# Pooled attention values on 64 zero-padded rows and four array quarters, copied out in four pieces

## The chip, the cores and the metric

The kernel runs on one core of one Trainium2 chip. The metric is the device time of one execution in microseconds (us); of several executions the median counts. The core has four engines that compute, each with its own queue of instructions: PE (the matmul array, whose weight loads are shown as an engine of their own, PEld), DVE (vector), ACT (activations and copies) and POOL. SP issues the transfers. Each engine works through its queue in the order of the program and waits at an instruction until what it needs is there.

## What is computed

Attention with two parts, and two dense layers behind it. The part that the change touches is the pooled one: queries, keys and values of 576 positions are averaged in groups of four to 144, full attention runs on these, and each result is repeated four times.

```python
q_d = q.reshape(B, H, Sd, factor, D).mean(axis=3)     # B, H = 8, 8; Sd = 144; D = 64
k_d = k.reshape(B, H, Sd, factor, D).mean(axis=3)
v_d = v.reshape(B, H, Sd, factor, D).mean(axis=3)
out_d = sm_attn(q_d, k_d, v_d)                        # softmax(q_d k_d^T / 8) v_d
out_up = np.repeat(out_d, factor, axis=2)
...
out_local = np.matmul(attn, v)                        # attention to positions at most 3 away
x = (out_up + out_local)                              # heads side by side: 4608 x 512
h = x @ w_in                                          # 512 -> 2048
return np.maximum(0.01 * h, h) @ w_out                # 2048 -> 512
```

## The kernel before

**The dense layers** take most of PE's time. The 4608 tokens are cut into chunks of 256, 320 and 384 (`CHUNKS`). For each chunk and each of 16 slices of the hidden layer, `up_proj` (L862) makes 12 matmuls into a bank `hp`, ACT and DVE form `gh` and `gl` from it (`leaky`, L872, L873, L875), and `down_proj` (L902) makes 12 matmuls into the four banks `acc0` to `acc3`.

**The attention** of batches 1 to 7 runs beside them. Two heads that lie in the partitions 0 to 63 and 64 to 127 of a tile are a head pair `c`; `pair(b, u)` handles the two head pairs `cs = 2u, 2u + 1`, so four heads, and runs 14 times (7 batches, 2 values of `u`). In the program below, `p` is the half of the partitions (which head of a head pair) and `i` the head pair of the two. The steps of `pair`:

- loads of queries and keys (`qk`) and of values (`vs`), with sums over four positions on DVE: `qk_d` (L499) and `v_d` (L511). The 144 pooled keys are held as three groups `kc` of 48; a head's group stands in 48 rows from row 0 or from row 64 of the tile. `KROWS` is 64 + 48 = 112.
- scores (L524): 12 matmuls over `qi`, `i`, `p`, each on 64 rows (the head's) and 64 columns of the array: rows by `p`, columns by `i`. All four quarters of the array are used in turn.
- softmax: maxima and reciprocals on DVE (L453, L454, L470, L471), exponentials and scaling on ACT (L463, L539), into `pds`. `pds` keeps 64 places for each group of 48 keys; the 16 places left over are zeros, written once by POOL at the start (L268).
- transposes (L548): nine per call, three for each `kc`, which put the keys on the partitions; ACT copies them to `ptd` (L551).
- values (L565): 12 matmuls over `i`, `kc`, `p`, each on the 48 rows of a head and 64 columns, which are the first 64 columns for all; the heads `p` have a bank each (`avs[p]`), the head pairs `i` stand side by side in it, 144 columns each.
- two ACT copies (L571), one for each bank, 64 partitions by 288, into `outd`. The sums that follow are `widen` (L808) and `landing` (L821, L828, L834, L836), which puts the attention's result into the input tiles `xh`, `xl` of the dense layers.

**Order.** All of this is written as generators. A planner (`Order`) keeps a time for each engine from stated costs and issues whichever step can start first; that fixes the program's order on each engine, and the chip runs it as written. The planner's costs of the steps in `pair` (`pe(1.1, ...)`, `op("ACT", 288, ...)`) are the same before and after the change, and one step issues all of its instructions together.

## Time and profile before

| | |
|---|---|
| median of three executions | 949.75 us (947.03 to 952.76) |
| the profiled execution | 951.45 us, its span 949.7 us |
| mean clock granted to PE | 0.987 of full speed |
| matmuls of scores, L524 | 336 records in 14 calls |
| matmuls of values, L565 | 336 records in 14 calls |

The profile tells, for one execution, when each instruction started and how long it took; the span is the time from its first to its last instruction. A matmul on 32-bit floats leaves two records, so that the 12 matmuls of a call are 24. Durations of matmuls include the way through the array and overlap, so that a row's duration is no distance: how long a block holds the engine is read from the start of its first matmul to the start of the next matmul behind it. Rows in the form `start, duration, engine line` are from the timeline, with the idle time before an instruction and what ended it in square brackets.

### The profile page before, as it was taken

To read this page: it belongs to the slowest core of one execution; us is meant where nothing else is said; L and a number is where in the kernel's file an instruction comes from. 1 tells how busy PE (TensorE), PEld (TensorE's weight loads), DVE (VectorE), ACT (ScalarE), POOL (GpSimd) and SP (SyncE) were. 2 spreads that over 40 slices of the span, in tenths; PEclk is the share of its full clock that TensorE was granted. 3 is DMA by queue.
4 is the path that set the end of the run, shared out by engine and by line. 5 is a ranking of instruction groups with operands and counts; after the bars stand their busy time and mean duration, and the time that the engine had idled before them with its cause. 6 is when DMAs were issued, how large, how long until landed. Compare 5 with 4: busy or idle time off the path is not lost.

```text
span 949.7 us, 16334 instructions
## 1 busy us (share of the span) xinstructions
PE 920.9 (97%) x6352; PEld 893.2 (94%) x6352; DVE 571.9 (60%) x897; ACT 414.2 (44%) x1133; POOL 610.1 (64%) x364
## 2 busy tenths in 40 slices
PE   6898999998899999999999999999999999999997
PEld 4688999898899999999999999999999999999997
DVE  4785866786676776568765776666665654311111
ACT  3777655553454454335543535343423423422211
POOL 4455867778767868787797687887888885100000
PEclk9699999999999999999999999999999999999999
DMA  9769556536333552333624452443332421000000
GB/s 243 240 210 330 174 158 209 178 109 192 124 112 97 181 161 82 111 119 123 199 82 131 129 168 84 128 130 96 113 99 77 149 60 51 34 1 1 34 1 34
DMA packets 60286, 117.60 MB, mean 124 GB/s; under 512 B 5472, under 2 KB 32864, under 8 KB 60208
## 3 DMA queue, kind: packets, MB, share of 16 engines
q1 hardware_dynamic: 60208, 116.55, 39.3%
q8 instruction: 50, 0.82, 0.4%
q14 instruction: 28, 0.23, 0.1%
HBM read 106.57 MB, written 9.96 MB: 123 GB/s over the span
## 4 chain that ended last, share of the span: by engine, by line
PE 90%; DMA 5%; DVE 2%; ACT 2%; issue 1%; SPq 0%; POOL 0%; DVEq 0%; POOLq 0%; ACTq 0%
PE acc L902 41%; PE hp L862 41%; PE pt L565 2%; PE pt L821 1%; PE pt L524 1%; DMA k<-in_w_in_dram 1%; PE pt L548 1%; DMA k<-in_kb_dram 1%; DMA su_vs<-in_vd_dram 1%; DMA w<-in_w_out_dram 1%; DMA vs<-in_vs_dram 1%; DVE s L729 0%; PE pt L624 0%; SPq L258 0%; ACT pds L463 0%
## 5 line engine op out<-in xcount | busy, mean ns | idle before, releaser
L723 POOL TENSOR_TENSOR prod<-q,k 128x1344 f32<-128x1344 f32 (+1 forms) x88 | 260.1, 2958 | 41.2 <-DMA k<-in_kb_dram 28.1
L784 POOL TENSOR_TENSOR prod<-v,s 128x1344 f32<-128x1344 f32 (+1 forms) x88 | 262.6, 2985 | 16.4 <-DMA v<-in_vb_dram 7.1
L872 ACT ACTIVATE gh<-hp 128x384 fp32r<-128x384 f32 (+2 forms) x208 | 97.4, 468 | 353.4 <-PE acc L902 334.4
L875 DVE TENSOR_TENSOR gl<-hp,gh 128x384 fp32r<-128x384 f32 (+2 forms) x208 | 108.8, 525 | 225.2 <-ACT hp L873 223.7
L862 PE MATMUL hp<-xh,w 128*128 128x384 f32 (+2 forms) x832 | 215.7, 327 | 0.0
L902 PE MATMUL acc<-gh,w 128*128 128x384 f32 (+2 forms) x832 | 215.5, 327 | 0.0
L862 PEld LDWEIGHTS hp<-xh,w 128*128 128x128 f32 x832 | 147.9, 188 | 1.2 <-issue 1.0
L902 PEld LDWEIGHTS acc<-gh,w 128*128 128x128 f32 x832 | 147.7, 188 | 1.2 <-issue 1.0
L862 PE MATMUL hp<-xh,wih 128*128 128x384 f32 (+2 forms) x416 | 139.7, 336 | 4.4 <-DVE gl L875 4.4
L790 DVE TENSOR_REDUCE xloc<-prod 128x192 f32<-128x1344 f32 (+1 forms) x88 | 130.0, 1477 | 13.9 <-POOL prod L784 13.8
L902 PE MATMUL acc<-gh,woh 128*128 128x384 f32 (+2 forms) x416 | 136.7, 328 | 1.4 <-ACT o L943 1.4
L729 DVE TENSOR_REDUCE s<-prod 128x21 f32<-128x1344 f32 (+1 forms) x88 | 130.1, 1479 | 11.4 <-POOL prod L723 11.2
L862 PE MATMUL hp<-xl,wih 128*128 128x384 f32 (+2 forms) x416 | 135.3, 325 | 0.8 <-DVE xl L836 0.8
L862 PE MATMUL hp<-xh,wil 128*128 128x384 f32 (+2 forms) x416 | 135.4, 326 | 0.0
L902 PE MATMUL acc<-gh,wol 128*128 128x384 f32 (+2 forms) x416 | 134.4, 323 | 0.4 <-POOL wol L341 0.4
L862 PE MATMUL hp<-xl,w 128*128 128x384 f32 (+2 forms) x416 | 134.8, 324 | 0.0
L902 PE MATMUL acc<-gl,w 128*128 128x384 f32 (+2 forms) x416 | 134.6, 324 | 0.0
L902 PE MATMUL acc<-gl,woh 128*128 128x384 f32 (+2 forms) x416 | 134.1, 322 | 0.0
L873 ACT ACTIVATE hp<-hp 128x384 f32<-128x384 f32 (+2 forms) x208 | 96.1, 462 | 0.0
L862 PEld LDWEIGHTS hp<-xh,wih 128*128 128x128 f32 x416 | 79.3, 191 | 7.9 <-DVE gl L875 5.6
L902 PEld LDWEIGHTS acc<-gh,woh 128*128 128x128 f32 x416 | 78.3, 188 | 3.0 <-ACT o L943 1.6
L862 PEld LDWEIGHTS hp<-xl,wih 128*128 128x128 f32 x416 | 79.3, 191 | 1.1 <-DVE xl L836 1.1
(172 smaller groups left out, 1228.7 us busy)
## 6 DMA issues: line engine op xcount, KB each, us to landing
k<-in_kb_dram SPq DMA_DIRECT2D x38, 576.0 KB, 4.3
v<-in_vb_dram SPq DMA_DIRECT2D x38, 576.0 KB, 4.8
qk<-in_qkt_dram SPq DMA_DIRECT2D x32, 576.0 KB, 5.8
vs<-in_vs_dram SPq DMA_DIRECT2D x56, 144.0 KB, 5.1
q<-in_qb_dram SPq DMA_DIRECT2D x38, 192.0 KB, 2.8
out_dram<-o SPq DMA_DIRECT2D x36, 192.0 KB, 2.0
w<-in_w_out_dram SPq DMA_DIRECT2D x6, 512.0 KB, 6.6
w<-in_w_in_dram SPq DMA_DIRECT2D x6, 512.0 KB, 7.7
```

What stands on the lines that cost most here:

```text
L524: nc.tensor.matmul(scs[p][outs, qi * SD:(qi + 1) * SD], qk_d[i][rows, qi * QB:qi * QB + 64], qk_d[i][rows, SD:2 * SD], start=True, stop=True)
L548: nc.tensor.transpose(tp[:KROWS, qi * 128:qi * 128 + KROWS], pds[:KROWS, qi, kc].rearrange("q p k -> q (p k)")[:, :KROWS], id_sb[:KROWS, : ...
L565: nc.tensor.matmul(avs[p][:64, i * SD:(i + 1) * SD], v_d[rows, i, kc], ptd[rows, kc, i], start=kc == 0, stop=kc == KC - 1)
L723: nc.gpsimd.tensor_tensor(out=prv, in0=q[:, p, a - j0:z - j0].unsqueeze(2).to_broadcast([128, n, W, D]), in1=view(k[:, p], (a - j0) * D, [ ...
L729: nc.vector.tensor_reduce(out=s[:, p, a - j0:z - j0], in_=prv, axis=AX.X, op=ALU.add)
L784: nc.gpsimd.tensor_tensor(out=prv, in0=view(v[:, p], a - j0, [[1, n], [nv, D], [1, W]]), in1=s[:, p, a - j0:z - j0].unsqueeze(2).to_broadc ...
L790: nc.vector.tensor_reduce(out=xl_t[:, :n, p], in_=prv, axis=AX.X, op=ALU.add)
L862: nc.tensor.matmul(hp[:, :n], wt[:, c], x[:, c], start=k == 0, stop=k == 3 * NC - 1)
L872: nc.scalar.activation(out=gh[:, :n], in_=hp[:, :n], func=AF.Prelu, alpha=0.01)
L873: nc.scalar.activation(out=hp[:, :n], in_=hp[:, :n], func=AF.Prelu, alpha=0.01)
L875: nc.vector.tensor_tensor(out=gl[:, :n], in0=hp[:, :n], in1=gh[:, :n].bitcast(F32), op=ALU.subtract)
L902: nc.tensor.matmul(acc[:, :n], wt[:, es], g[:, :n], start=f == f0 and j == 0, stop=f == f1 - 1 and j == 2)
```

## The change

The values' matmuls run on 64 rows for each head in place of 48: `v_d`, `vs` and `ptd` have 128 partitions, the rows 48 to 63 and 112 to 127 hold zeros (`vs` is cleared at the start, and the places that `pds` leaves free are carried through the transposes). The second head pair's results go to the columns 64 to 127 of the array, so to the partitions 64 to 127 of the banks, in place of 144 further columns of the first 64 partitions. The loop over `kc` is the outer one now, and within it the four quarters follow in the order in which the scores use them. Since a bank's results stand on two halves of its partitions, four copies of 64 x 144 replace the two of 64 x 288.

```diff
-    vs = const.tile([KROWS, KC, D, FAC], F32, name="vs")
+    vs = const.tile([128, KC, D, FAC], F32, name="vs")
...
-                v_d = sb(s_vd, [KROWS, 2, KC, D], F32)
+                v_d = sb(s_vd, [128, 2, KC, D], F32)
...
-        ptd = sb(s_pt, [KROWS, KC, 2, 3, QB], F32)
+        ptd = sb(s_pt, [128, KC, 2, 3, QB], F32)
...
-                nc.tensor.transpose(tp[:KROWS, qi * 128:qi * 128 + KROWS], pds[:KROWS, qi, kc].rearrange("q p k -> q (p k)")[:, :KROWS],
+                nc.tensor.transpose(tp[:, qi * 128:qi * 128 + KROWS], pds[:KROWS, qi, kc].rearrange("q p k -> q (p k)"),
                                     id_sb[:KROWS, :KROWS])
...
-                           in_=tp[:KROWS, :384].rearrange("k (a i q) -> k a i q", a=3, i=2)[:, :, :, :QB])
+                           in_=tp[:, :384].rearrange("k (a i q) -> k a i q", a=3, i=2)[:, :, :, :QB])
...
-        for i in range(2):
-            for kc in range(KC):
+        for kc in range(KC):
+            for i in range(2):
                 for p in range(2):
-                    rows = slice(64 * p, 64 * p + QB)
-                    nc.tensor.matmul(avs[p][:64, i * SD:(i + 1) * SD], v_d[rows, i, kc], ptd[rows, kc, i],
+                    rows = slice(64 * p, 64 * p + 64)
+                    nc.tensor.matmul(avs[p][64 * i:64 * i + 64, :SD], v_d[rows, i, kc], ptd[rows, kc, i],
                                      start=kc == 0, stop=kc == KC - 1)
...
-            nc.scalar.copy(out=outd[b][64 * p:64 * p + 64, cs[0]:cs[1] + 1], in_=avs[p][:64, :2 * SD].rearrange("p (c s) -> p c s", c=2))
+            for i, c in enumerate(cs):
+                nc.scalar.copy(out=outd[b][64 * p:64 * p + 64, c], in_=avs[p][64 * i:64 * i + 64, :SD])
```

The change adds one line, so what stands behind L571 has a number higher by one (L862 is L863 then, the copies are L572).

On PE, around the values of the first call, the program before reads so (`hp` is the bank of a hidden slice, `xh` and `xl` the layer's input, `wih` and `wil` its weights, `pt` the two banks of the values):

```order
L862 MATMUL hp<-xl_599,wih_70 128x320
L862 MATMUL hp<-xh_598,wil_71 128x320
L565 MATMUL pt<-ptd,v_d 64x144 x12
L862 MATMUL hp<-xh_598,wih_70 128x320
L862 MATMUL hp<-xl_599,wih_70 128x320
```

and the changed one, at the same place:

```order
L863 MATMUL hp<-xl_599,wih_70 128x320
L863 MATMUL hp<-xh_598,wil_71 128x320
L565 MATMUL pt<-ptd,v_d 64x144 x12
L863 MATMUL hp<-xh_598,wih_70 128x320
L863 MATMUL hp<-xl_599,wih_70 128x320
```

Nothing moved against its neighbours; only the order within the twelve, which the row puts together, and their place in the array are others.

On ACT, around the copies of the second call, the program before reads so:

```order
L551 COPY ptd<-pt 112x3x2x48
L872 ACTIVATE gh<-hp 128x320
L873 ACTIVATE hp<-hp 128x320
L745 ACTIVATE s<-s 128x2x14
L571 COPY outd<-pt 64x288 x2
L749 ACTIVATE st_l<-st_l 128x2x2
L872 ACTIVATE gh<-hp 128x320
```

and the changed one:

```order
L551 COPY ptd<-pt 128x3x2x48
L873 ACTIVATE gh<-hp 128x320
L874 ACTIVATE hp<-hp 128x320
L746 ACTIVATE s<-s 128x2x14
L572 COPY outd<-pt 64x144 x4
L750 ACTIVATE st_l<-st_l 128x2x2
L873 ACTIVATE gh<-hp 128x320
```

The four copies stand where the two stood, ahead of the same small step of the local attention's softmax (L749, then L750) and of the next `gh`; the copy to `ptd` spans 128 partitions in place of 112.

## The prediction, made before the changed kernel ran

> **What bounds the kernel now.** I read the page first: the busy shares, then the chain that ended last.

> ```profile
> PE 920.9 (97%) x6352; PEld 893.2 (94%) x6352; DVE 571.9 (60%) x897; ACT 414.2 (44%) x1133; POOL 610.1 (64%) x364
> ...
> PE 90%; DMA 5%; DVE 2%; ACT 2%; issue 1%; SPq 0%; POOL 0%; DVEq 0%; POOLq 0%; ACTq 0%
> ```

> PE is busy for 97% of the span and makes 90% of the chain; no other engine passes 64%. So a microsecond taken off PE's queue counts if nothing else then keeps PE waiting. Busy time by stage (columns: stretch and its length, then the busy time of PE, PEld, DVE, ACT and POOL) and the first row of PE's waits behind the first 62 us (total, times, longest) tell where it does wait:

> ```profile
> 174.00:304.00 130.00, 122.54 (x979) 118.75 (x979) 91.68 (x147) 61.81 (x188) 97.89 (x59) 0.97 0.43 135
> ...
> 446.00:820.00 374.00, 374.00 (x2328) 368.52 (x2327) 241.43 (x335) 153.30 (x401) 290.86 (x156) 1.00 0.36 111
> ```

> ```profile
> PE hp L862 <- DVE gl L875: 4.2, 3, 3.1
> ```

> From 446 to 820 us PE never stops. Between 174 and 304 us it idles 7.5 us, and the longest wait, 3.1 us, falls into that stretch, as does one of 2.9 us that is taken up below.

> **The block that changes.** The rows of the grouped view give the totals:

> ```profile
> L565 PE MATMUL pt<-ptd,v_d 48*64 48x144 f32 x336 | 23.6, 287 | 0.0
> ...
> L524 PE MATMUL pt<-qk_d 64*64 64x144 f32 x336 | 14.7, 302 | 2.9 <-DVE xl L836 2.9
> ```

> The timeline gives the distances, first the values of one call, then the scores of one call, each with the matmul behind it:

> ```profile
> 249.23 1.69 PE L565 MATMUL pt<-ptd,v_d 48*64 48x144 f32 x24
> 250.85 0.41 PE L862 MATMUL hp<-xh,wih 128*128 128x320 f32 x1
> ...
> 270.17 0.97 PE L524 MATMUL pt<-qk_d 64*64 64x144 f32 x24
> 271.07 0.42 PE L902 MATMUL acc<-gh,woh 128*128 128x320 f32 x1
> ```

> Both blocks are 24 records of 64 columns by 144, on 32-bit floats. The values hold PE for 250.85 - 249.23 = 1.62 us, the scores for 271.07 - 270.17 = 0.90 us. What differs is the place in the array: the values use two quarters (rows by `p`, always the first 64 columns), the scores four (rows by `p`, columns by `i`). The rows say the same per round: 24 records two at a time are 12 rounds, four at a time 6, and 0.72 us over 6 rounds is 0.12 us a round, which is 1.44 of 1.62 us for 12; the 0.18 us left are the way in and out, 0.18 us in both.

> The change gives the values the scores' rows, columns, banks and order (`kc`, `i`, `p` in place of `qi`, `i`, `p`): four successive matmuls in four different quarters, the two row halves in different banks. Only the sums differ: the values add three groups `kc` into the same place, the scores write each place once. But the values of before also add three groups into one place, and that does not spoil their rounds of 0.12 us. I therefore take 0.90 us for the new block: **-0.72 us for each of 14 calls, -10.1 us of PE time.** The bounds of a block are 0.90 us and, if nothing overlaps that does not now, 1.62 us. That a head takes 64 rows in place of 48 costs nothing by these rows: the scores have 64.

> **The other edits.** Transposes: nine per call, 126 in all, write 128 partitions in place of 112; they still stream 112 columns. The timeline has three of them, and three of `landing` that stream 128:

> ```profile
> 204.30 0.45 PE L548 MATMUL pt<-id_sb,pds 112*112 112x112 f32 x3
> 204.52 0.36 PE L862 MATMUL hp<-xh,w 128*128 128x256 f32 x1
> ...
> 205.32 0.49 PE L821 MATMUL pt<-id_sb,xloc 128*128 128x128 f32 x3
> 205.57 0.36 PE L902 MATMUL acc<-gh,woh 128*128 128x256 f32 x1
> ```

> 0.22 us for three of 112 and 0.25 us for three that are 128 on both sides bound it: 0 to 42 x 0.03 = 1.3 us. I take 0, since what streams keeps its 112.

> Copies: two of 64 x 288 become four of 64 x 144.

> ```profile
> L571 ACT COPY outd<-pt 64x288 f32<-64x288 f32 x28 | 11.0, 393 | 25.4 <-PE pt L565 25.0
> ...
> L433 ACT COPY outd<-hp 128x144 f32<-128x144 f32 x2 | 0.6, 280 | 1.5 <-PE hp L448 1.5
> ```

> ```profile
> 250.95 0.81 ACT L571 COPY outd<-pt 64x288 f32<-64x288 f32 x2 [2.98 <-PE pt L565]
> 252.53 0.44 ACT L872 ACTIVATE gh<-hp 128x320 fp32r<-128x320 f32 x1 [0.77 <-PE acc L902]
> ```

> A copy of 144 columns took 0.280 us (L433), so four take 1.12 to 1.15 us in place of 0.81: +0.34 us a call, 4.8 us of ACT in all. If a copy of 64 x 144 cost as much as one of 64 x 288, it would be +0.81 us a call. Behind the copies on ACT stands the next `gh` (L872), for which DVE (`gl`) and then PE (L902) wait. In the rows shown ACT is done at 251.76 and idles 0.77 us until that `gh`, and ACT idles 2.98 us ahead of the copies; so either price is mostly hidden, and I take 0. Without that cover it would be 0.34 x 14 = 4.8 us. The copies also start 0.72 us earlier, so `outd` is complete 0.38 us sooner than now by the first price. The copies to `ptd` (L551) get 16 more partitions and no more columns; in the two grouped rows the price goes by columns (280 ns for 144 on 128 partitions, 393 ns for 288 on 64), so I take 0. The larger clearing of `vs` lies in POOL's first instructions. No transfer changes size or place in SP's queue.

> **How much of 10.1 us reaches the end.** PE's saving ahead of a wait counts only if what ends the wait comes earlier too. For the wait of 2.9 us I followed the timeline back:

> ```profile
> 227.11 0.79 ACT L943 COPY o<-acc 128x256 f32<-128x256 f32 x2 [2.53 <-PE acc L902]
> 227.80 0.24 ACT L745 ACTIVATE s<-s 128x42 f32<-128x42 f32 x1
> 228.07 0.20 DVE L747 TENSOR_REDUCE st_l<-s 128x6 f32<-128x42 f32 x1 [1.94 <-ACT s L745]
> 231.48 0.42 DVE L836 TENSOR_TENSOR xl<-pt,xh 128x256 fp32r<-128x256 f32 x1
> 232.04 1.71 PE L524 MATMUL pt<-qk_d 64*64 64x144 f32 x22 [2.86 <-DVE xl L836]
> ```

> PE waits for DVE (`xl`, until 231.90), DVE had waited for ACT, and ACT for PE's own `acc` at 227.1. The wait hangs on PE's pace: what PE has gained before it, the wait's end gains too. Not so where a load stands between. Such a place follows one of the values blocks:

> ```profile
> 178.62 1.69 PE L565 MATMUL pt<-ptd,v_d 48*64 48x144 f32 x24
> ...
> 179.59 1.06 SPq L258 DMA_DIRECT2D vs<-in_vs_dram  x2
> ...
> 186.21 0.95 DVE L511 TENSOR_REDUCE v_d<-vs 112x192 f32<-112x768 f32 x1 [3.02 <-PE acc L902]
> 187.08 1.54 DVE L790 TENSOR_REDUCE xloc<-prod 128x192 f32<-128x1344 f32 x1
> 188.77 0.52 PE L821 MATMUL pt<-id_sb,xloc 128*128 128x128 f32 x3
> ```

> The load of `vs` was issued at 179.6, before that block ended (178.62 + 1.62 = 180.24), DVE sat idle 3.02 us ahead of the sum over it, and PE's transposes started 0.15 us behind DVE's `xloc` (188.62): this block's 0.72 us runs into that wait and is lost. The same two DVE rows bound the sum to `v_d` (L511) on 128 partitions in place of 112: between 0 and what the sum of 1344 columns on 128 partitions took beyond it, 1.54 - 0.95 = 0.59 us, 28 times, on an engine that is busy 60%. I take 0, since a column took no more on 128 partitions (1.54 / 1344 = 1.15 ns) than on 112 (0.95 / 768 = 1.24 ns).

> Of the other 13 blocks, I expect all to reach the end: **13 x 0.72 = 9.4 us.** The view of L565 by stretch has the blocks ahead of 304 us, 24 records each:

> ```profile
> 62.00:174.00 112.00, 5.06 (x72) 4.26 (x72) 1.00 0.66 209
> 174.00:304.00 130.00, 5.06 (x72) 4.26 (x72) 0.97 0.43 135
> ```

> The worst I can argue is that of these six nothing gets through, because the waits up to 304 us swallow it: 8 x 0.72 = 5.8 us. The best is 10.1.

> The sum stands against the profiled execution: span 949.7 - 9.4 = 940.3 us, with 1.8 us around it 942.1. That execution (951.45) was 1.7 us above the median of the three; the same saving against the median gives 949.75 - 9.4 = **940.3 us**, 1.0% less.

> **Rivals.**

> *The columns do not overlap* (the change does not do what it says): two quarters at a time, as now, 1.62 us a block, about 949.7 us. Against it: the scores' 0.90 us with the same quarters. For it: only that sums into one place on four quarters appear nowhere in this trace.

> *The waits swallow it*: 5.8 us get through, 943.9 us. For it: 7.5 us of idle PE between 174 and 304. Against it: the chain shown at 232.

> *The copies take it back*: ACT's 0.34 us a call delays `gh`, and PE waits: 9.4 - 4.8 = 4.6 us gained, 945.1 us; at 0.81 us a call 11.3 us would be lost against 9.4 won. Against it: ACT is busy 44%. [...]

> *Weight loads come into the open* (the one that ends slower): two matmuls of one row half now follow each other in different columns. If the second's weight load could not run beside the first's matmul, 12 of the 24 records would each show a load:

> ```profile
> L565 PEld LDWEIGHTS pt<-ptd,v_d x336: 129/133/133, 81.0 to 650.8; 48*64 48x64 f32 x168
> ```

> At 0.133 us that is 12 x 0.133 = 1.6 us on 0.90, so 2.5 us a block, 14 x 0.88 = 12.3 us slower: 962.0 us. It decides from 0.06 us a load (0.72 / 12). [...] Against it: the scores follow each other in the same way, and their block takes 0.90 us, loads included.

> **Chances.** The forecast 0.80; swallowed by waits 0.08; no overlap 0.05; copies 0.04; loads 0.03. A measurement of this kernel can tell about 0.5% from no change (4.7 us, so from 945.0 us down). Faster by more: the forecast and most of the second, 0.86. Within 0.5%: no overlap, the copies, the rest of the second, 0.11. Slower by more: the loads, 0.03. The range reaches down to all 14 blocks (939.6) and up to the swallowed case (943.9), both widened by about 2 us since the three executions lie up to 3.0 us from their median: 937.5 to 945.5.

> **What would show it.** In the changed profile, L565 from its first start to the next matmul's: 0.90 us right, 1.62 no overlap, more the loads. PE's busy time lower by about 10 us. The copies (L572) at 0.28 us, and no engine waiting for them. The wait at 232 as long as before, and starting about 3 us earlier; the transposes at 188.8 with some 0.6 us more of waiting. The prediction is wrong if PE's block shrinks and the end does not move by 13 times as much.

## The result, and the profile after

| | before | after |
|---|---|---|
| median of seven executions each, on one chip | 949.75 us (947.03 to 952.81) | 943.96 us (942.44 to 945.90) |
| ratio, with its 95% interval | | 0.9927 (0.9906 to 0.9948) |
| the profiled execution, its span | 951.45, 949.7 us | 945.54, 943.8 us |
| mean clock granted to PE in it | 0.987 | 0.981 |
| mean of all executions of this study, on several chips | 950.83 us (65) | 944.05 us (14) |

The change makes the kernel 5.8 us faster by the medians, and 6.8 us by the means of all executions (with 1.0 us, twice its standard error, on either side). 9.4 us were forecast: the sign is right and the time lies in the range, but over a quarter of the gain is missing by the means, and more than a third by the medians.

The blocks first. From the timeline of the changed kernel, the values of one call, the matmul behind them and their copies, and under them the weight loads of the first call's values:

```profile
249.83 0.97 PE L565 MATMUL pt<-ptd,v_d 64*64 64x144 f32 x24
250.72 0.41 PE L863 MATMUL hp<-xh,wih 128*128 128x320 f32 x1
250.84 1.14 ACT L572 COPY outd<-pt 64x144 f32<-64x144 f32 x4 [2.28 <-PE pt L565]
...
80.49 0.70 PEld L565 LDWEIGHTS pt<-ptd,v_d 64*64 64x64 f32 x24 [0.19 <-issue]
```

The block holds PE for 250.72 - 249.83 = 0.89 us, as forecast. Four copies take 1.14 us.

Now the waits of PE behind the first 62 us (total, times, longest), the first three rows:

```profile
PE hp L863 <- DVE gl L876: 3.8, 2, 3.3
PE acc L903 <- ACT o L944: 3.1, 1, 3.1
PE pt L524 <- DVE xl L837: 2.8, 1, 2.8
```

The second row is what has changed: one wait of 3.1 us for ACT's copy of an output (`o`), where the kernel before waited 1.38 us. The timeline shows that place, first in the kernel before, then in the changed one:

```profile
90.44 0.95 DVE L511 TENSOR_REDUCE v_d<-vs 112x192 f32<-112x768 f32 x1 [0.88 <-DMA vs<-in_vs_dram]
92.03 0.67 ACT L339 CAST w<-w 128x512 fp32r<-128x512 f32 x1 [1.10 <-DVE w L325]
92.59 0.65 ACT L943 COPY o<-acc 128x256 f32<-128x256 f32 x2
93.02 0.41 PE L902 MATMUL acc<-gh,woh 128*128 128x320 f32 x1 [1.38 <-ACT o L943]
```

```profile
90.15 0.31 PE L863 MATMUL hp<-xh,wil 128*128 128x320 f32 x1
90.95 0.95 DVE L511 TENSOR_REDUCE v_d<-vs 128x192 f32<-128x768 f32 x1 [2.58 <-DMA vs<-in_vs_dram]
92.54 0.65 ACT L339 CAST w<-w 128x512 fp32r<-128x512 f32 x1 [2.81 <-DVE w L325]
93.10 0.64 ACT L944 COPY o<-acc 128x256 f32<-128x256 f32 x2
93.52 0.63 PE L903 MATMUL acc<-gh,woh 128*128 128x320 f32 x1 [3.06 <-ACT o L944]
94.22 0.47 PE L903 MATMUL acc<-gh,wol 128*128 128x320 f32 x1
94.49 0.47 PE L903 MATMUL acc<-gh,woh 128*128 128x320 f32 x1
```

Read backwards: PE waits for ACT's `o`, ACT for the weights' conversion (L339), that for DVE (L325), and DVE sits in front of its sum L511 until a load of `vs` lands. PE is done with its last matmul at 90.46 (90.15 + 0.31), earlier than before (93.02 - 1.38 = 91.64), but the load is not earlier. And then the matmuls of 320 columns follow each other at 94.49 - 94.22 = 0.27 us, where 0.15 is usual (251.12 to 251.27 us in the same profile). The view by stretch says why (its last three columns are the granted clock, the DMA share and GB/s):

```profile
91.80:92.40 0.60, 0.00 (x0) 0.00 (x0) 0.60 (x2) 0.00 (x0) 0.23 (x1) 1.00 1.09 428
92.40:92.60 0.20, 0.00 (x0) 0.00 (x0) 0.20 (x2) 0.06 (x1) 0.20 (x1) 0.55 1.02 404
92.60:99.20 6.60, 5.68 (x21) 5.68 (x22) 3.89 (x3) 3.74 (x9) 5.63 (x3) 0.50 1.01 349
99.20:99.40 0.20, 0.20 (x3) 0.20 (x2) 0.00 (x0) 0.20 (x1) 0.00 (x0) 0.88 0.47 159
```

From about 92.4 to 99.2 us PE is granted half its clock; in the kernel before it has 1.00 there. Half speed from 93.52 to 99.2 is 2.8 us of work lost, by this estimate, more than three blocks' gain (e2 below, with the same wait and the full clock, comes to the second block in 2.6 us less). By the DMA share of 1.01 to 1.09 the 16 DMA engines are busy throughout from 91.8 to 99.2 us.

To see where the gain arrives, I measure from block to block. Starts of the first two blocks of values, before and after (the sixth are at 249.23, in the prediction, and at 249.83, above):

```profile
80.96 1.69 PE L565 MATMUL pt<-ptd,v_d 48*64 48x144 f32 x24
...
122.49 1.69 PE L565 MATMUL pt<-ptd,v_d 48*64 48x144 f32 x24
```

```profile
80.50 0.97 PE L565 MATMUL pt<-ptd,v_d 64*64 64x144 f32 x24
...
124.71 0.96 PE L565 MATMUL pt<-ptd,v_d 64*64 64x144 f32 x24
```

Read in the same way, with the executions of the experiments below that have the same order of work:

| execution | 1st to 2nd block, us | 2nd to 6th | 6th to end | wait at 93 | clock, 88 to 104 us |
|---|---|---|---|---|---|
| before | 41.53 | 126.74 | 700.5 | 1.38 | 1.00 |
| e1, before again | 42.17 | 127.02 | 700.5 | 2.88 | 1.00 |
| e6, padding alone | 41.47 | 125.17 | 700.4 | 2.18 | 1.00 |
| after | 44.21 | 125.12 | 694.0 | 3.06 | 0.79 |
| e2, after again | 41.63 | 124.55 | 694.0 | 3.06 | 1.00 |
| e5, after timed | 45.01 | 125.20 | 694.0 | 3.80 | 0.79 |
| e7, eight copies | 43.09 | 124.75 | 694.0 | 3.17 | 0.89 |
| e11, 48 rows | 45.23 | 123.97 | 694.0 | 4.78 | 0.79 |
| forecast of the change | -0.72 | -2.16 | -6.48 | | |
| measured (mean of five less mean of three) | +2.1 | -1.6 | -6.5 | | |

The last nine blocks bring 9 x 0.72 = 6.48 us to within 0.1 us, in every execution. The second and the third bring theirs too: from the second block to the fourth it is 56.1 us in each of the three profiles of the old values and 54.7 in each of the five of the new. From the fourth to the sixth nothing can be told: 70.6, 70.9 and 69.0 us with the old values, 70.4, 69.8, 70.5, 70.1 and 69.3 with the new. The first one brings nothing, and 2 us on average are lost on top.

The load of `vs` ends the wait at 93 us not in this one profile alone. The sum L511 waits for it in all eight, and in all five profiles of the new values and in two of the three of the old ones, PE starts again 2.56 to 2.58 us behind the start of that sum (in the rows above 93.02 - 90.44 and 93.52 - 90.95), in e6 3.06 us: the steps between the two take the same time whenever the load comes.

### The profile page after: what moved, and what is told of

Same layout as the page of the kernel before. It is cut to its first block, busy times and chain, and to the rows that moved or that the text cites. A ratio compares the mean times of both kernels' runs of the same rounds, so it can differ in the third digit from the quotient of the medians.

```text
span 943.8 us, 16357 instructions
## 1 busy us (share of the span) xinstructions
PE 914.0 (97%) x6352; PEld 887.5 (94%) x6352; DVE 572.1 (61%) x897; ACT 418.9 (44%) x1161; POOL 608.8 (65%) x364
## 4 chain that ended last, share of the span: by engine, by line
PE 92%; DMA 3%; DVE 2%; ACT 2%; SPq 0%; issue 0%; DVEq 0%
PE acc L903 42%; PE hp L863 42%; PE pt L822 1%; PE pt L565 1%; PE pt L548 1%; PE pt L524 1%; DMA k<-in_w_in_dram 1%; DMA su_vs<-in_vd_dram 1%; DMA out_dram<-o 1%; DMA vs<-in_vs_dram 1%; DVE s L730 0%; PE pt L625 0%; ACT pds L463 0%; SPq L258 0%; PE pt L666 0%
## 5 line engine op out<-in xcount | busy, mean ns | idle before, releaser
L724 POOL TENSOR_TENSOR prod<-q,k 128x1344 f32<-128x1344 f32 (+1 forms) x88 | 260.3, 2960 | 43.8 <-DMA k<-in_kb_dram 30.9
L863 PE MATMUL hp<-xh,w 128*128 128x384 f32 (+2 forms) x832 | 215.7, 327 | 0.0
L903 PE MATMUL acc<-gh,w 128*128 128x384 f32 (+2 forms) x832 | 215.6, 327 | 0.0
L863 PEld LDWEIGHTS hp<-xh,w 128*128 128x128 f32 x832 | 147.9, 188 | 1.2 <-issue 1.0
L903 PEld LDWEIGHTS acc<-gh,w 128*128 128x128 f32 x832 | 147.7, 188 | 1.2 <-issue 0.8
L863 PE MATMUL hp<-xh,wih 128*128 128x384 f32 (+2 forms) x416 | 140.5, 338 | 3.8 <-DVE gl L876 3.8
L903 PE MATMUL acc<-gh,woh 128*128 128x384 f32 (+2 forms) x416 | 137.8, 331 | 3.1 <-ACT o L944 3.1
L863 PE MATMUL hp<-xl,wih 128*128 128x384 f32 (+2 forms) x416 | 136.2, 327 | 0.8 <-DVE xl L837 0.8
L863 PE MATMUL hp<-xh,wil 128*128 128x384 f32 (+2 forms) x416 | 136.3, 328 | 0.0
L903 PE MATMUL acc<-gh,wol 128*128 128x384 f32 (+2 forms) x416 | 135.5, 326 | 0.4 <-POOL wol L341 0.4
L903 PE MATMUL acc<-gl,woh 128*128 128x384 f32 (+2 forms) x416 | 135.2, 325 | 0.0
L863 PE MATMUL hp<-xl,w 128*128 128x384 f32 (+2 forms) x416 | 134.8, 324 | 0.0
L903 PE MATMUL acc<-gl,w 128*128 128x384 f32 (+2 forms) x416 | 134.7, 324 | 0.0
L863 PEld LDWEIGHTS hp<-xh,wih 128*128 128x128 f32 x416 | 80.2, 193 | 6.7 <-DVE gl L876 4.5
L903 PEld LDWEIGHTS acc<-gh,woh 128*128 128x128 f32 x416 | 79.4, 191 | 4.7 <-ACT o L944 3.3
L863 PEld LDWEIGHTS hp<-xl,wih 128*128 128x128 f32 x416 | 80.1, 193 | 1.1 <-DVE xl L837 1.1
```

Source lines behind the costliest of these rows:

```text
L724: nc.gpsimd.tensor_tensor(out=prv, in0=q[:, p, a - j0:z - j0].unsqueeze(2).to_broadcast([128, n, W, D]), in1=view(k[:, p], (a - j0) * D, [ ...
L863: nc.tensor.matmul(hp[:, :n], wt[:, c], x[:, c], start=k == 0, stop=k == 3 * NC - 1)
L903: nc.tensor.matmul(acc[:, :n], wt[:, es], g[:, :n], start=f == f0 and j == 0, stop=f == f1 - 1 and j == 2)
```

## The experiments

Theory A: PE comes to the wait at 93 us earlier, what ends it is a transfer, so the first block's gain is idle time; and the longer idle time lowers PE's clock behind it. Theory B: what the first profile shows at 93 us is scatter between executions. Differences that are given with a +- are between means, with twice the standard error.

**e1 and e2, both kernels once more, for their profiles**

> The kernel before once more, for its profile alone. Theory A (the changed kernel comes to the wait for the output copy at 93 us 0.72 us earlier, a load of vs ends that wait, and PE's granted clock falls because the wait got long): the wait of L902 behind L862 at 93 us is again 1.2 to 1.8 us here, and the granted clock in the 5 us behind it again 1.00. Theory B (what happened at 93 us is scatter between executions): wait and clock may come out differently here, for instance 3 us and 0.5.

> The changed kernel once more, for its profile alone. Theory A: the wait of L903 at 93 us is again at least 0.6 us longer than in the kernel before (2.0 to 3.2 us), with a lower granted clock (about 0.5) in the few us behind it. Theory B: wait and clock come out as in the kernel before, 1.4 us and 1.00, and the span is then about 2.5 us shorter than the first profile of the changed kernel (943.8), so 941.3.

From the timelines, first e1, then e2, and e2's view by stretch and busy row:

```profile
92.29 0.42 PE L902 MATMUL acc<-gh,woh 128*128 128x320 f32 x1 [2.88 <-ACT o L943]
```

```profile
93.12 0.41 PE L903 MATMUL acc<-gh,woh 128*128 128x320 f32 x1 [3.06 <-ACT o L944]
```

```profile
92.00:96.00 4.00, 2.88 (x19) 2.88 (x20) 4.00 (x4) 3.35 (x7) 4.00 (x3) 1.00 1.06 383
96.00:100.00 4.00, 4.00 (x30) 4.00 (x29) 3.15 (x6) 1.97 (x4) 3.64 (x3) 1.00 0.87 266
...
PE 910.9 (97%) x6352; PEld 884.1 (94%) x6352; DVE 572.3 (61%) x897; ACT 418.8 (45%) x1161; POOL 609.0 (65%) x364
```

Both theories get half. The old values can wait 2.88 us here too, so the first profile's 1.38 us was the short end. And the same 3.06 us of idle time as in the first profile were followed by the full clock, so that the same idle time is not followed by the lower clock each time (the last section shows with what the lower clock went). Without the lower clock, e2 goes from block to block in 41.63 us, as the old values do (41.5 to 42.2): the 0.72 us are swallowed, and nothing is lost on top. Its span is 940.3 us, and its PE is busy 10.0 us less than before (920.9), which is the forecast's 10.1.

**e3, the first block as before**

```diff
+        old = (b, u) == (BANDED, 0)
+        for x in range(2 if old else KC):
+            for y in range(KC if old else 2):
...
+                    (i, kc), rows = (x, y) if old else (y, x), slice(64 * p, 64 * p + 64)
+                    to_ = avs[p][:64, i * SD:(i + 1) * SD] if old else avs[p][64 * i:64 * i + 64, :SD]
```

> The changed kernel, in which the first of the 14 blocks of values, at 80 us, has the two quarters of before (on the 64 padded rows) and its two copies. This block holds PE for 1.62 us in place of 0.90. Theory A: PE comes to the wait at 93 us 0.72 us later, the wait is 2.3 us in place of 3.06, it ends where it ended, so the 0.72 us cost nothing: 943.2 to 944.0 us; if the clock behind it no longer falls, up to 1.8 us less, 942.2. Theory B: the 0.72 us arrive at the end, 943.96 + 0.72 = 944.7 us.

Median 942.07 us (938.22 to 942.98, five), ratio to before 0.9907 (0.9885 to 0.9928). Its timeline and its view by stretch:

```profile
92.54 0.63 PE L907 MATMUL acc<-gh,woh 128*128 128x320 f32 x1 [2.17 <-ACT o L948]
```

```profile
92.40:95.60 3.20, 3.06 (x11) 3.06 (x12) 2.88 (x3) 2.09 (x6) 3.20 (x3) 0.50 1.05 358
...
95.80:97.00 1.20, 1.20 (x10) 1.20 (x9) 0.03 (x1) 0.27 (x2) 1.20 (x1) 1.00 1.05 415
```

With one block slower by 0.72 us the kernel is not slower; the means say 2.6 +- 1.9 us faster than the changed kernel. Theory B's 944.7 us is out. The wait is 2.17 us (2.3 expected by theory A), and the lower clock lasts 3.4 us in place of 6.8.

**e4 and e12, the wait filled: twelve matmuls done twice ahead of it, in the changed kernel and in the one before**

```diff
+            for k in range(3 * NC if i == 12 else 0):
+                wt, x = ((wh, xh), (wh, xl), (wl, xh))[k % 3]
+                nc.tensor.matmul(hp[:, :n], wt[:, k // 3], x[:, k // 3], start=k == 0, stop=k == 3 * NC - 1)
             od.spawn(-10, leaky(i, n, s_h, hp, t))
```

> The changed kernel with 12 matmuls more: the twelve matmuls of a hidden slice (L863) that stand ahead of the wait at 93 us are done a second time into the same bank with the same result, about 1.75 us of work for PE in a wait of 3.06 us. If the idle time brings the lower clock (theory A): the rest of the wait is about 1.3 us, the granted clock behind it stays near 1.00 as in the kernel before, matmuls of 320 columns follow each other at 0.15 us in place of 0.27, and 1.8 us are won at the end although PE does more: 942.2 us. If the clock falls for another reason (the loads, the time since the start): clock about 0.5 behind the wait as in the changed kernel, 944.0 us. If the added work delays gh: later than 944, up to 945.7 us.

> The kernel before with the same 12 matmuls more ahead of the wait at 93 us. In three executions of the old values that wait was 1.4 to 2.9 us and the clock behind it stayed 1.00. If the missing 2.5 to 3 us of the forecast are the first block's 0.72 us and the lower clock that the longer wait brings in the changed kernel alone: the added 1.75 us of work lie in the wait, nothing or little is won here (949.5 to 951.5 us, a ratio of 0.998 to 1.001), and the change is worth 9 to 10 us between the two filled kernels (940.35 was measured for the other). If the filling helps the old values as much as the new (the lower clock has nothing to do with the change): about 947.5 us, a ratio of 0.997, and the change is worth 7 us here too.

The changed kernel, filled: median 940.35 us (940.09 to 942.08, five), ratio 0.9902 (0.9883 to 0.9921). The kernel before, filled: 951.70 us (949.58 to 952.87, twelve), ratio 1.0009 (0.9992 to 1.0026). Timeline and clock, e4 and then e12:

```profile
91.98 0.41 PE L906 MATMUL acc<-gh,woh 128*128 128x320 f32 x1 [0.77 <-ACT o L947]
...
88.00:104.00 16.00, 15.23 (x103) 14.82 (x102) 13.06 (x17) 8.96 (x20) 13.72 (x10) 1.00 0.90 315
```

```profile
92.07 0.41 PE L905 MATMUL acc<-gh,woh 128*128 128x320 f32 x1 [0.43 <-ACT o L946]
...
88.00:104.00 16.00, 15.57 (x105) 15.26 (x105) 13.06 (x17) 9.29 (x20) 14.13 (x10) 1.00 0.86 299
```

About 1.75 us of work that nobody needs make the changed kernel 3.1 +- 1.2 us faster; in its profile the wait shrinks to 0.77 us and the clock stays at 1.00. The same work in the kernel before wins nothing (+0.5 +- 0.9 us). Between the two filled kernels the change is worth 10.4 +- 1.1 us. The place fits too: from the first block to the second the filled kernels take 41.10 us (e4) and 41.48 (e12), the unfilled ones of the table 43.8 and 41.7 on average, so that the filling takes 2.7 us out of this stretch with the new values and 0.2 with the old. So what is missing from the forecast is lost at the wait at 93 us and behind it, and it is lost with the new values only. The single profiles say less about the rest of the 10.4 us: from the second block to the sixth e4 and e12 differ by 3.9 us (124.01 and 127.92), more than all four blocks there can give; both wait for 2.8 us and more at two places, and the half clock lasts 3.4 us in the one and 10.2 in the other. The filled kernel is the fastest of the study; it beats both kernels.

**e5, the changed kernel timed again**

> The changed kernel once more, timed beside the kernel before on the chip of these runs. If all but one of the 14 blocks reach the end on average and the first profile had bad luck with its clock (a granted clock of 0.5 from 92.4 to 99.2 us, where another execution of the same kernel kept 1.00 behind the same idle time): 8.5 to 9.5 us under the kernel before, a ratio of 0.990 to 0.991. If about 3.5 us are lost in each execution: 5.8 us under it, 0.994.

Median 944.11 us (940.99 to 947.32, six) against 950.33, ratio 0.9916 (0.9885 to 0.9948): 6.2 us by the medians, 8.0 by the ratio. On its own it doesn't decide; its profile shows 3.80 us of waiting at 93 and the lower clock for 6.8 us again.

**e6, the padding alone**

```diff
-        for kc in range(KC):
-            for i in range(2):
+        for i in range(2):
+            for kc in range(KC):
...
-                    nc.tensor.matmul(avs[p][64 * i:64 * i + 64, :SD], v_d[rows, i, kc], ptd[rows, kc, i],
+                    nc.tensor.matmul(avs[p][:64, i * SD:(i + 1) * SD], v_d[rows, i, kc], ptd[rows, kc, i],
```

(and the two copies of before)

> The padding of the change alone: 64 rows for each head, tiles of 128 partitions, transposes onto 128 partitions, but the values in the two quarters, the order of loops and the two copies of before. As predicted the padding costs nothing: the block of L565 holds PE for 1.62 us, and the time is that of the kernel before within 2 us. If the padding has a price (transposes 1.3 us in all, sums to v_d on 128 partitions, larger copies to ptd) that a faster block has hidden in the changed kernel: 1 to 4 us slower than before.

Median 950.49 us (946.16 to 956.13, twelve), ratio 0.9988 (0.9965 to 1.0012). The grouped view:

```profile
L511 DVE TENSOR_REDUCE v_d<-vs 128x192 f32<-128x768 f32 x28 | 26.6, 950 | 16.5 <-DMA vs<-in_vs_dram 11.0 <-PE pt L565 5.4
L565 PE MATMUL pt<-ptd,v_d 64*64 64x144 f32 x336 | 23.6, 287 | 0.0
L548 PE MATMUL pt<-id_sb,pds 112*128 112x112 f32 x126 | 19.5, 260 | 1.3 <-DVE st_l L751 0.7 <-ACT pds L539 0.4 <-ACT su_pt L653 0.3
```

64 rows cost what 48 cost (L565: 23.6 us, as before), the sums to `v_d` take 950 ns where they took 949, and the transposes onto 128 partitions 260 ns where they took 263. From the sixth block to the end it takes 700.4 us, as before. So no price of the padding shows, as the prediction had it; the timed difference (-0.3 +- 1.7 us to the mean of before) could not tell one of 1 us.

**e7, eight copies**

```diff
-                nc.scalar.copy(out=outd[b][64 * p:64 * p + 64, c], in_=avs[p][64 * i:64 * i + 64, :SD])
+                for s0 in (0, SD // 2):
+                    nc.scalar.copy(out=outd[b][64 * p:64 * p + 64, c, s0:s0 + SD // 2], in_=avs[p][64 * i:64 * i + 64, s0:s0 + SD // 2])
```

> The changed kernel with eight copies of 64 x 72 in place of four of 64 x 144. By the rows of 64 x 288 (393 ns) and 64 x 144 (280 ns) a copy of 72 columns takes about 0.22 us, so 1.8 us for eight in place of 1.13: 0.65 us more of ACT in each of 14 calls, twice what the change added. If ACT's copies are hidden: the time of the changed kernel within 1.5 us. If what was lost of the forecast went to the copies (about 3.5 us for 0.32 us a call): 7 us slower than the changed kernel.

Median 943.24 us (940.88 to 946.44, six), ratio 0.9909 (0.9874 to 0.9945); against the changed kernel -0.6 +- 2.0 us. The grouped view:

```profile
L573 ACT COPY outd<-pt 64x72 f32<-64x72 f32 x112 | 18.5, 213 | 15.5 <-PE pt L565 14.9
...
248.41 1.37 ACT L573 COPY outd<-pt 64x72 f32<-64x72 f32 x8 [2.28 <-PE pt L565]
```

A copy took 213 ns, but eight in a row only 1.37 us (the second row is the timeline's), not 1.8: they overlap. So the experiment is weaker than meant, 0.23 us more a call in place of 0.65. It still speaks: 14 x 0.23 = 3.2 us would have come out at the end if nothing hid the copies, and -0.6 +- 2.0 us leaves no room for that; from the sixth block to the end it takes the 694.0 us of the changed kernel.

**e8, the old order of loops in the new quarters**

```diff
-        for kc in range(KC):
-            for i in range(2):
+        for i in range(2):
+            for kc in range(KC):
```

> The changed kernel with the loops in the order of before (i, kc, p): the four quarters are used, but only two of them in turn, first all six matmuls of one head pair, then all six of the other. If four different quarters in a row make the block short: 1.62 us a block as before, L565 at about 80 us, and some 949 us. If it is enough that the results lie in different quarters, whatever the order: 0.90 us and the time of the changed kernel.

One execution, 946.17 us. The timeline, a block and the matmul behind it:

```profile
247.72 1.26 PE L565 MATMUL pt<-ptd,v_d 64*64 64x144 f32 x24
248.91 0.41 PE L863 MATMUL hp<-xh,wih 128*128 128x320 f32 x1
```

1.19 us: neither answer. Of the 0.73 us between 1.62 and 0.89, the place of the results gives 0.43, and the order in which the quarters follow each other the other 0.30. PE overlapped some matmuls of different quarters here that are not neighbours in the program. The starts of the block's 24 records in the trace show how: they come two at a time up to 0.30 us, four at a time from there to 0.73 (one such group every 0.12 us), then two at a time again. So, as far as starts can tell, the second head pair's matmuls begin at 0.31 us, when six of the first pair's twelve records have begun: inside this block PE did not start its matmuls in the strict order of the program.

**e9 and e10, one load earlier, in the kernel before and in the changed one**

```diff
-            if v_d is None:
+            if v_d is None and (b, u) != (BANDED, 1):
...
                 tv = yield from load(vs[64 * p:64 * p + QB], vs3[b - BANDED, c, p], 148e3, sv.t)
+            if v_d is None:
+                s_vd = yield from slot("v_d")
+                v_d = sb(s_vd, [128, 2, KC, D], F32)
```

(in e9 with `KROWS` in place of 128)

> The kernel before with one load earlier: the values vs of the second call's first head pair, for which DVE's sum L511 waits at 90 us, are asked for ahead of the wait for the tile v_d instead of behind it, so that the load stands 12 places further ahead in SP's queue. If that load ends PE's wait at 93 us (1.4 to 2.9 us in three executions): the wait falls under 1 us, and the time is 1 to 3 us under the kernel before, 948 to 949.5 us. If something else ends it (ACT or the weights' loads): the wait stays, and the time is that of the kernel before.

> The changed kernel with the same load earlier, and the same order on PE as the one above. If the load at 93 us swallowed the first block's 0.72 us and brought the lower clock: no wait over 1 us at 93, granted clock 1.00 from 88 to 104 us, the first block's 0.72 us arrive at the second block, and the difference to the kernel above is 12 or 13 blocks, 8.6 to 9.4 us, so about 939.5 us. If the loss has another place: the difference stays at 5.8 to 7 us.

e9: median 952.25 us (951.01 to 955.32, nine), ratio 1.0020 (1.0003 to 1.0038). e10: 945.65 us (941.90 to 948.30, six), ratio 0.9948 (0.9928 to 0.9967). Timelines, e9 and then e10:

```profile
90.17 0.69 ACT L946 COPY o<-acc 128x256 f32<-128x256 f32 x2 [2.08 <-DMA out_dram<-o]
90.60 0.42 PE L905 MATMUL acc<-gh,woh 128*128 128x320 f32 x1 [1.79 <-ACT o L946]
...
232.00 0.66 PE L824 MATMUL pt<-id_sb,xloc 128*128 128x128 f32 x2 [7.41 <-DVE st_l L744]
```

```profile
92.15 0.71 ACT L947 COPY o<-acc 128x256 f32<-128x256 f32 x2 [1.21 <-DMA out_dram<-o]
92.58 0.42 PE L906 MATMUL acc<-gh,woh 128*128 128x320 f32 x1 [0.93 <-ACT o L947]
```

Part of theory A falls here: the load of `vs` was not alone. With it out of the way, ACT waits in front of the same copy until an earlier output has been stored (`out_dram`), and PE still waits 1.79 and 0.93 us. So there are at least two transfers that can be the last here. Both times miss what was expected of the earlier load (948 to 949.5 and 939.5 us): moving it also changed the planner's order later on, which brings a wait of 7.4 us at 232 (7.2 in e10) and a half clock of 10 and 14 us around it. With a full clock at 93 in both, the pair of profiles differs by 1.27 us from the first block to the second (38.88 us in e9, 37.61 in e10), which has room for the first block's 0.72 us; the shorter wait makes up the rest. The timed difference, 7.2 +- 2.2 us, doesn't tell 9 from 6.8.

**e11, 48 rows in four quarters**

```diff
-                    rows = slice(64 * p, 64 * p + 64)
+                    rows = slice(64 * p, 64 * p + QB)
```

> The changed kernel with the matmuls on 48 rows for each head, as before, but in the four quarters (the tiles stay padded). If the quarters alone make the block short: L565 holds PE for 0.90 us and the time is that of the changed kernel, 942 to 945 us. If the 64 rows are needed for four at a time: about 1.62 us a block and some 950 us.

One execution, 943.99 us; the grouped view:

```profile
L565 PE MATMUL pt<-ptd,v_d 48*64 48x144 f32 x336 | 13.5, 291 | 0.0
```

13.5 us in all, as for 64 rows (L565 of the changed kernel has 13.5, 291 too). The quarters alone make the block short; the 16 rows of zeros are not needed for it, and cost nothing either.

## Why the prediction came out as it did

- **The block, 1.62 to 0.90 us: right.** 0.89 us at 250, the same in all 14 calls; PE's busy time falls by 10.0 us in e2; in the first profile after it falls by 6.9 (920.9 to 914.0), because matmuls at half clock take longer (0.47 us in place of 0.31 in the rows above). Sums into one place on four quarters overlap like the single ones of the scores (0.89 us and 0.90 us a block). The rivals without overlap (1.62 us) and with weight loads in the open (2.5 us) are out: 24 loads took 0.70 us, within the block's 0.89. In the block at 249.83 the load for the other column half on the same rows starts 0.01 us behind the first matmul, whose record lasts 0.33 us, and in the kernel before (249.23) the next load for the very same quarter starts 0.05 us behind it, and the next matmul there only at 0.17 us. So in both blocks loads ran beside a matmul on the same rows.
- **Padding at nothing: right** as far as e6 can tell. **Copies: right**, 274 ns each (0.280 expected) and 1.14 us for four; in the changed profile no engine waits for them, and e7 shows them hidden. The copies' rival is out.
- **The block at 178 us, lost in the wait behind it: right in part.** The 0.6 us of further waiting at the transposes do not show in the first profile; PE waits there for 0.40 us in e2, 0.55 in e7 and 1.03 in e3, and hardly in the others. From this block to the next it takes 41.6 to 42.0 us with the old values and 41.1 to 41.8 with the new, 0.3 us less on average. (The prediction's row puts DVE's 3.02 us of waiting down to PE; the trace has the second load of `vs` land at 186.09, 0.12 us ahead of the sum, so that the load fits, as the prediction read it.)
- **The wait at 232 as long as before: right**, 2.80 us against 2.86, since PE's own work ends it:

```profile
230.94 0.42 DVE L837 TENSOR_TENSOR xl<-pt,xh 128x256 fp32r<-128x256 f32 x1
231.47 0.72 PEld L524 LDWEIGHTS pt<-qk_d 64*64 64x64 f32 x22 [3.04 <-issue]
231.51 0.96 PE L524 MATMUL pt<-qk_d 64*64 64x144 f32 x22 [2.80 <-DVE xl L837]
```

  But PE goes on from it only 0.5 us earlier than before (231.51 against 232.04) in place of 3, because of what went at 93.
- **"Of the other 13 blocks, I expect all to reach the end: 13 x 0.72 = 9.4 us" is the step that failed.** The mechanism (each block's gain reaches the end unless a wait ahead takes it) is right, the second and third block and nine of nine from 249 us on show it; the term was too large, 6.8 +- 1.0 us measured. By the prediction's own last sign (the block shrinks and the end does not move by 13 times as much) it was wrong here. I looked for transfers that end a wait from 174 us on, and found the one at 188. The first block has one 13 us behind it, at 93. The profile before had it: PE 1.38 us idle for `o`, and on DVE a wait for the load of `vs`. There the first block's 0.72 us are lost. That the time lies in the range all the same is owed to the range's upper end, which the rival "the waits swallow it" had set; the prediction gave that rival 0.08.
- **What I had not thought of** is that idle time can cost more than itself. The profile before shows that as well: the clock of 0.97 from 174 to 304 us in the prediction's row is two stretches of 3.4 us at half clock, from 231.9 and from 242.1 us, at its two waits of 2.86 and 3.10 us. The new values wait 3.06 to 4.78 us at 93 where the old waited 1.38 to 2.88 (five and three executions of the table), and four of those five then ran 3.4 to 6.8 us at half clock, of those three none. On average that is the +2.1 us of the table in place of -0.72.
- The rival "the waits swallow it" named 943.9 us, closer to the median than the forecast, but by luck: it put the loss into the 7.5 us of idle PE between 174 and 304 us and let none of six blocks through. In fact the second and third came through, and the first stretch lost more than its block.

What stays open is why the wait at 93 is longer by 1.4 us on average, and not by 0.72. The load that ends it was asked for 0.1 to 1.0 us behind the start of the first block in the five profiles of the new values, and from 0.9 us ahead of it to 0.3 behind it in the three of the old. In the two where it was asked for at the same time (0.34 us behind in e1, 0.36 in the first profile after) the wait ended 13.57 and 13.02 us behind the block's start, so not later with the new values. The longer waits therefore go with later loads; whether the change has a hand in these or only the scatter of eight executions isn't shown.

## What to carry to other kernels

Follow each saving forward to the next wait behind it, from the first call on, and ask what ends that wait: where it is a transfer, the saving turns into idle time (the first block's 0.72 us here), and where the DMA engines are busy throughout (a share of 1.06 in e9 and 1.03 in e10 from 88.0 to 92.6 us), taking away the last transfer can uncover the next: PE still waited 1.79 us in e9 and 0.93 in e10. A saving ahead of such a wait can even cost time, when a lower clock follows the longer idle stretch, as it did in four of the five profiles of the new values (0.50 for 3.4 to 6.8 us); work of no use in the wait was worth 3.1 +- 1.2 us in e4. For small 32-bit matmuls, look at which quarters of the array follow each other: the same 24 records took 1.62 us in two quarters and 0.89 in four.

## What the runs showed of the hardware

```profile
89.01:92.42 3.41, 1.45 (x10) 1.19 (x9) 1.47 (x2) 0.72 (x2) 2.30 (x3) 1.00 1.03 380
92.42:95.84 3.42, 2.32 (x9) 2.32 (x10) 3.42 (x3) 2.18 (x5) 3.42 (x2) 0.50 1.04 389
```

```profile
88.45:91.87 3.42, 1.61 (x12) 1.35 (x10) 1.31 (x2) 0.89 (x2) 2.33 (x3) 1.00 1.05 370
91.87:95.28 3.41, 2.16 (x15) 2.16 (x15) 3.41 (x3) 2.86 (x7) 3.41 (x2) 1.00 1.05 392
```

  Busy for 1.45 of 3.41 us, the clock fell; for 1.61 of 3.42 (0.47), between the two bounds, where either happened, it did not. Behind waits of less than 2.0 us at 93 (before 1.38, e9 1.79, e10 0.93, e4 0.77, e12 0.43) the clock never fell; from 2.17 us on it fell in five of nine executions.
- Executions differ by microseconds before the first block of values has run: it started between 77.3 (e6) and 81.7 us (e10), and for one and the same program, the kernel before, at 80.96 and at 78.72. Two profiles are therefore compared from one mark in the program to the next; their spans alone would have given any gain between 0.6 us (e6 against the first profile after) and 9.4 us (the first before against e2).
